# Reordering a state-space/FFN mix kernel: the second state's input projection before the first FFN output, one phase tile moved to VectorE, a constant for the warm-up

## Chip, cores, metric

One core of one Trainium2 chip. The metric is device time in microseconds (us) of the slowest (here the only) core; medians over several executions are quoted. Engine names in the profile: PE is TensorE, PEld its weight loads, DVE is VectorE, ACT is ScalarE, POOL is GpSimd, SP is SyncE; a "q" behind a name means that engine's instruction queue.

## The reference

```python
g = sigmoid((x * gate_w).sum(-1))                 # x: 2048 tokens x 448
Lam_bar = exp(dt * Lam); B_bar = (Lam_bar - 1) / Lam * B        # 448 complex states
h[t] = Lam_bar * h[t-1] + x[t] @ B_bar.T          # sequential over 2048 tokens
a = 2 * real(h @ C.T) + x * Dskip
b = silu(x @ w1) @ w2                             # 448 -> 1792 -> 448
out = g * a + (1 - g) * b                         # bfloat16
```

The kernel works on even and odd tokens apart (1024 pairs), in four chunks of 512 tokens for the FFN ("FFN1(c)" is x@w1 of chunk c, "FFN2(c)" the four 128-token rows q = 0..3 of silu(..)@w2) and in four tiles of states ("tile pt", "Bu(pt)" is its projection of x). The complex recurrence is turned into a real scan by multiplying with sine and cosine tables over the pair index. A table needs a *phase*: index times frequency, less its nearest integer.

## The kernel before

Each engine executes its own list in order; a tracker inserts semaphore waits from the declared reads and writes. So the order in which the program emits operations is the order on each engine. These are the parts that the change touches.

```python
        def phases(pt):                                   # GpSimd, two operations of 128x1024 f32
            f2 = "f2s" if pt == 3 else "f2"
            X, RR = phase(pt), G[:, pt % 2, :]
            T.op("pool", lambda e: e.tensor_scalar(X, IOTA[:, :], c1(f2, pt), 0.0, ALU.mult, ALU.add), ...)
            T.op("pool", lambda e: e.tensor_scalar(RR, X, 1.0, MAGIC, ALU.mult, ALU.add), ...)

        def phases2(pt):                                  # VectorE, one operation with two tensor inputs
            T.op("dve", lambda e: e.scalar_tensor_tensor(X, RR, MAGIC, X, ALU.subtract, ALU.subtract), ...)
        # ... (cut)
        ptt("lr", ...); ptt("li", ...); pts("nli", ...)   # 128x4 coefficients on VectorE; then "lis"
        phases(0)
        phases(3)
        phases2(0)
        phases(2)
        T.op("dve", ... tensor_copy(BT[0:64, 3, :], BT[64:128, 3, :]) ...)
        T.op("dve", ... tensor_copy(BR, BT[..., 384:448]) ...)          # TensorE needs BR for Bu(3)
        phases2(3)
        phases(1)
        swap_xr("dve", 1, 0)
        phases2(2)
        phases2(1)
        # ... (cut)
        def ffn2(c, q):                                   # 14 matmuls into one PSUM bank
            # c == 0: VectorE evicts it, bank * gate ratio + x * Dskip;  other chunks: ScalarE evicts
        # ... (cut: the main order)
        settle(); run(g2, 4)        # ScalarE: last SiLU, gate sums
        run(t3)                     # ScalarE: sine and cosine table of tile 3
        run(g2)                     # ScalarE: the other gate sums
        run(s0, 1)                  # VectorE: tile 0, turn and two scans
        run(g3)                     # VectorE: gate values for the first 1024 tokens
        for q in range(4):
            ffn2(0, q)              # TensorE; VectorE evicts
        run(s3, 1)                  # VectorE: a step of tile 3 (needs its tables)
        # ... (cut)
        bu(1, 0)
        bu(1, 1)
        for i, _ in enumerate(ffn1(2)):
```

## Time and profile before

Median 139.33 us (139.32 to 139.85). The profiled run took 139.70 us, of which 137.9 us are the span that the profile shows.

| engine | busy us | share of the span |
|---|---|---|
| PE | 133.1 | 97% |
| DVE | 121.7 | 88% |
| ACT | 94.8 | 69% |
| POOL | 31.1 | 23% |

The whole list of waits of TensorE in the kernel before (who waited, for whom; total us, times, longest):

```profile
PE ps L441 <- DVE Q L246: 1.0, 1, 1.0
PE ps L346 <- DVE IOTA L740: 0.9, 1, 0.9
PE ps L399 <- DVE XT L459: 0.2, 1, 0.2
```

The first and the last belong to the start. The middle one is the only hole later on. The timeline of TensorE around it (start us, us, engine, line, operation, output and input names, count; in brackets the idle time before it and what ended that):

```profile
36.75 10.77 PE L732 MATMUL ps<-W,AT 128*128 128x448 bf16 x56
47.45 2.55 PE L346 MATMUL ps<-XT,BT 64*128 64x512 bf16 x22
50.90 3.20 PE L346 MATMUL ps<-XT,BT 64*128 64x512 bf16 x28 [0.90 <-DVE IOTA L740]
```

FFN2(0) is the x56, Bu(1) follows. The 22 matmuls that start at 47.45 need 22 x 0.108 = 2.4 us, the next starts at 50.90: about 1.06 us is lost (the bracket says 0.90 because the end of a matmul is modelled). It waits for a PSUM bank that VectorE evicts late, since on VectorE the gate values and the evictions stand behind tile 0's two scans:

```profile
43.70 4.46 DVE L826 TENSOR_TENSOR_SCAN G<-P,Q 128x1024 f32<-128x1024 f32 x2
...
49.02 2.41 DVE L740 SCALAR_TENSOR_TENSOR IOTA<-ps,GT,XN 128x448 bf16<-128x448 f32 x4
```

The early phases in the kernel before, from the timelines of GpSimd and then of VectorE:

```profile
13.04 1.05 POOL L544 TENSOR_SCALAR G<-FP 128x1024 f32<-128x1024 f32 x1
14.26 2.07 POOL L542 TENSOR_SCALAR Q<-IOTA,P 128x1024 f32<-128x1024 f32 x1 [0.17 <-DVE P L600]
```

```profile
14.12 1.23 DVE L549 SCALAR_TENSOR_TENSOR FP<-G,FP 128x1024 f32<-128x1024 f32 x1
...
17.83 1.00 DVE L608 COPY BR<-BT 128x512 bf16<-128x512 bf16 x1
```

GpSimd's tensor_scalars of this size take 1.04 to 1.16 us when nothing holds them; the one that starts at 14.26, while a VectorE subtraction runs, takes 2.07. The copy of BR ends at 18.83; TensorE wants it at 19.61.

### The profile page before, as it was taken

What the parts mean: (1) busy time and instruction counts of PE and PEld (TensorE: products, weight loads), DVE (VectorE), ACT (ScalarE), POOL (GpSimd) and SP (SyncE); (2) the same over time, 40 slices, a digit from 0 to 9 for tenths busy, and PEclk for the clock granted to TensorE, in tenths of its full rate; (3) what the DMA queues carried; (4) which work ended last, traced back from release to release, by engine and by line L of the source; (5) the groups of instructions that cost most, each with busy time, mean ns of one, the idle gap of its engine ahead of it and who ended that gap; (6) DMA issues with size and microseconds to landing.
All of it is one profiled execution on the core that took longest, in us unless ns stands there. A gap on an engine that the chain in (4) does not pass through costs nothing.

```text
span 137.9 us, 2403 instructions
## 1 busy us (share of the span) xinstructions
PE 133.1 (97%) x957; PEld 65.4 (47%) x957; DVE 121.7 (88%) x151; ACT 94.8 (69%) x154; POOL 31.1 (23%) x36
## 2 busy tenths in 40 slices
PE   7999999999999979999999999999999999999992
PEld 7444444444455424444554444445555555555561
DVE  1269576999999999999999999999999999999763
ACT  0459899979999955899999258797214437789100
POOL 7105999950000000099940000000000000000000
PEclk9999999999999999999999999999999999999999
DMA  3999389899881500020200000000000000222124
GB/s 102 341 223 294 67 162 161 126 384 373 166 171 31 118 0 0 20 61 0 61 15 0 5 0 0 0 5 0 0 0 0 0 5 28 72 100 67 60 74 133
DMA packets 24321, 11.80 MB, mean 86 GB/s; under 512 B 16564, under 2 KB 23864, under 8 KB 24312
## 3 DMA queue, kind: packets, MB, share of 16 engines
q1 hardware_dynamic: 22724, 10.57, 31.5%
q10 hardware_dynamic: 1588, 1.11, 2.7%
q8 instruction: 7, 0.11, 0.4%
q14 instruction: 2, 0.02, 0.0%
HBM read 5.51 MB, written 1.84 MB: 53 GB/s over the span
## 4 chain that ended last, share of the span: by engine, by line
PE 60%; DVE 21%; SPq 12%; DMA 3%; issue 3%; DVEq 0%
PE ps L732 23%; PE ps L346 23%; PE ps L931 14%; SPq L231 10%; DVE G L826 3%; DVE Q L789 3%; DVE HS L792 3%; DMA XT<-in_A_x_dram 3%; SPq L228 2%; DVE G L792 2%; DVE FP L549 2%; DVE XN L590 2%; DVE CO L582 2%; DVE IOTA L740 1%; DVE FP L792 1%
## 5 line engine op out<-in xcount | busy, mean ns | idle before, releaser
L732 PE MATMUL ps<-W,AT 128*128 128x448 bf16 x224 | 42.9, 353 | 0.0
L346 PE MATMUL ps<-XT,W1E 64*128 64x512 bf16 x325 | 39.7, 376 | 0.0
L732 PEld LDWEIGHTS ps<-W,AT 128*128 128x128 bf16 x224 | 21.7, 98 | 21.2 <-ACT AT L417 0.8
L417 ACT ACTIVATE AT<-ps 128x1024 bf16<-128x1024 f32 x28 | 27.9, 1024 | 1.8 <-PE ps L346 1.8
L346 PEld LDWEIGHTS ps<-XT,W1E 64*128 64x128 bf16 x325 | 17.0, 94 | 19.1 <-DVE W1E L475 0.3
L346 PE MATMUL ps<-XT,BT 64*128 64x512 bf16 x168 | 20.0, 377 | 0.9 <-DVE IOTA L740 0.9
L745 ACT ACTIVATE BT<-ps,GT 128x448 bf16<-128x448 f32 x8 | 5.1, 633 | 13.1 <-PE ps L732 13.1
L778 ACT ACTIVATE VE<-ps 128x1024 bf16<-128x1024 f32 (+1 forms) x9 | 7.5, 836 | 8.8 <-PE ps L346 8.8
L346 PEld LDWEIGHTS ps<-XT,BT 64*128 64x128 bf16 x168 | 8.0, 94 | 11.3 <-DVE IOTA L740 1.4
L636 POOL TENSOR_TENSOR P<-P 128x4 f32<-128x4 f32 x5 | 5.6, 1122 | 29.1 <-DVE P L643 28.8
L931 PE MATMUL ps<-CO,VE 128*128 128x448 bf16 (+1 forms) x63 | 11.6, 332 | 0.0
L931 PE MATMUL ps<-CO,HS 128*128 128x448 bf16 x56 | 11.6, 353 | 0.0
L826 DVE TENSOR_TENSOR_SCAN G<-P,Q 128x1024 f32<-128x1024 f32 (+1 forms) x6 | 11.3, 1919 | 0.0
L346 PE MATMUL ps<-XR,W1E 64*128 64x512 bf16 x25 | 9.2, 376 | 0.0
L931 PEld LDWEIGHTS ps<-CO,VE 128*128 128x128 bf16 x63 | 6.1, 98 | 4.7
L792 DVE SCALAR_TENSOR_TENSOR HS<-VE,P,G 128x512 bf16<-128x512 bf16 (+1 forms) x10 | 8.1, 856 | 0.2
L931 PEld LDWEIGHTS ps<-CO,HS 128*128 128x128 bf16 x56 | 5.5, 98 | 5.1
L792 DVE SCALAR_TENSOR_TENSOR G<-VE,P,HS 128x1024 f32<-128x1024 bf16 (+1 forms) x5 | 7.5, 1495 | 0.1
L784 ACT ACTIVATE HS<-ps 128x1024 bf16<-128x1024 f32 (+1 forms) x9 | 7.5, 833 | 0.1
L789 DVE TENSOR_TENSOR Q<-G,COS 128x2048 bf16<-128x2048 f32 (+1 forms) x4 | 7.0, 1756 | 0.1
L789 DVE TENSOR_TENSOR Q<-G,SIN 128x2048 bf16<-128x2048 f32 (+1 forms) x4 | 7.0, 1750 | 0.0
L923 ACT ACTIVATE ps<-XN 128x448 f32<-128x448 bf16 x9 | 4.6, 539 | 1.4 <-DVE OT L955 1.4
(117 smaller groups left out, 186.6 us busy)
## 6 DMA issues: line engine op xcount, KB each, us to landing
W<-in_B_w_dram SPq DMA_DIRECT2D x1, 1568.0 KB, 11.9
XN<-in_A_x_dram SPq DMA_DIRECT2D x1, 896.0 KB, 7.9
out_dram<-OT SPq DMA_DIRECT2D x8, 112.0 KB, 1.7
out_dram<-TMPS SPq DMA_DIRECT2D x7, 112.0 KB, 1.7
W1E<-in_B_w_dram SPq DMA_DIRECT2D x3, 224.0 KB, 4.5
HS<-HS SPq DMA_DIRECT2D x4, 128.0 KB, 2.3
W1E<-in_B_w_dram SPq DMA_DIRECT2D x1, 384.0 KB, 6.1
XN<-in_A_x_dram SPq DMA_DIRECT2D x1, 384.0 KB, 5.9
```

The costliest lines, as they stand in the source:

```text
L231: return T.dma("sp", lambda e: e.dma_start_transpose(dst, src), reads=reads, writes=[key, *also], group=group)
L346: ins = pe.matmul(ps[:, bank, :], w(p, j), xh(odd, h, j, p), start=start and j == js[0], stop=stop and j == js[-1])
L417: T.op("act", lambda e: e.activation(a[:, fb:fb + n, :], ps[:, bank:bank + n, :], AF.Silu), reads=[f"ps{bank + i}" for i in range(n)], wri ...
L636: T.op("pool", lambda e: e.tensor_tensor(col(o), a, b, op), reads=ra, writes=[o])
L732: ins = pe.matmul(ps[:, bank, 0:D], a[:, fb, q * 128:(q + 1) * 128], W2[:, fb, :], start=(first and fb == 0), stop=(fb == NFB - 1), skip_g ...
L745: T.op("act", lambda e: e.activation(bs(tile), ps[:, bank, 0:D], AF.Copy, scale=sc), reads=[f"ps{bank}", "GT2" if h else "GRI"], writes=ks)
L778: T.op("act", lambda e: e.activation(VE[:, m0:m0 + n, hs], ps[:, b0:b0 + n, :], AF.Copy), reads=pe_, writes=[f"V{m}_{h}" for m in ms])
L784: T.op("act", lambda e: e.activation(HS[:, m0:m0 + n, 8 + h * 512:8 + (h + 1) * 512], ps[:, b1:b1 + n, :], AF.Copy), reads=po_, writes=[f" ...
L789: T.op("dve", lambda e: e.tensor_tensor(o, a, b, op), reads=reads, writes=writes)
L792: T.op("dve", lambda e: e.scalar_tensor_tensor(o, a, s, b, ALU.mult, ALU.add), reads=reads, writes=writes)
L826: T.op("dve", lambda e, c=c, init=init: e.tensor_tensor_scan(G[:, c, w], rb, Q1[:, c, w], init, ALU.mult, ALU.add), reads=[f"Q1{c}", "rr", ...
L931: ins = pe.matmul(ps[:, bank, c], state(kt, odd, m), CO[:, m, c], start=False, stop=(m == YB[-1]), skip_group_check=True)
```

## The change

Its intent: while VectorE is still in its scans, let TensorE do Bu(1), which ScalarE evicts, and do FFN2(0) after it, so that FFN2's banks need not be free so early. So that VectorE need not evict all four rows late, two rows (q = 2, 3) are *seeded*: ScalarE writes the scaled x into the bank first, the matmuls add to it, and ScalarE evicts. GpSimd is relieved of one of four tiles of phases. The warm-up matmuls read a constant that the program's preamble has written on GpSimd (at 0.36 us in the profile after), so that they need not wait for VectorE's memset. The diff is shortened; cuts are in brackets.

```diff
-NWARM = 24
+NWARM = 26
-        T.op("dve", lambda e: e.memset(Q1[:, 0, 0:128], 0.0), writes=["Q10"])
+        ones = nc.const_aps.tensor(1.0, [128, 128], BF16)
-                    ins = pe.matmul(ps[:, 7, 0:128], Q1[:, 0, 0:128], Q1[:, 0, 0:128], ...)
+                    ins = pe.matmul(ps[:, 7, 0:128], ones, ones, ...)
@@ phases (G's half by GP = (0, 0, 1, 1) instead of pt % 2)
-        def phases(pt):
+        def phases(pt, eng="pool"):
@@ order of phases, coefficients and copies
+        phases(0)
+        phases(2, "dve")
+        phases2(2)
+        phases(3)
+        phases2(0)
+        phases(1)
         ptt("lr", ...) ... lis
-        phases(0)
-        phases(3)
-        phases2(0)
-        phases(2)
+        ptt("rr", ...)
         (copies of BT and BR)
         phases2(3)
-        phases(1)
+        phases2(1)
         swap_xr("dve", 1, 0)
-        phases2(2)
-        phases2(1)
@@ ffn2
-            first = c != 2
+            first = c != 2 and (c, q) not in ((0, 2), (0, 3))
@@ main order
+        bu(1, 0)
+        run(g2, 2)
+        bu(1, 1)
+        run(g2, 1)
         settle()
-        run(g2, 4)
+        run(g2, 1)
         run(t3)
-        run(g2)
         run(s0, 1)
+        run(g3, 1)
+        for q in (2, 3):
+            ffn2_seed(q, q, 0)
+        ffn2(0, 0)
+        run(g2)
         run(g3)
-        for q in range(4):
-            ffn2(0, q)
         run(s3, 1)
+        for q in (1, 2, 3):
+            ffn2(0, q)
         (cut)
-        bu(1, 0)
-        bu(1, 1)
```

More of the change, by code (lines that the diff above doesn't have):

```diff
@@ L440, in mm @@
                 for _ in range(n):
-                    ins = pe.matmul(ps[:, 7, 0:128], Q1[:, 0, 0:128], Q1[:, 0, 0:128], start=True, stop=True)
+                    ins = pe.matmul(ps[:, 7, 0:128], ones, ones, start=True, stop=True)
                 return ins
-            T.op("pe", mm, reads=["Q10"], writes=["ps7"])
+            T.op("pe", mm, writes=["ps7"])
         warm(NWARM)
@@ L530, in gated_mix @@
         first = next(first)
-        ptt("rr", col("mag"), col("mag"), ALU.mult, ["mag"])
+        GP = (0, 0, 1, 1)
         def phase(pt):
@@ L537, in phase @@
             return Q3[:, :, :].rearrange("p a b -> p (a b)").bitcast(F32)
-        def phases(pt):
+        def phases(pt, eng="pool"):
             f2 = "f2s" if pt == 3 else "f2"
-            X, RR = phase(pt), G[:, pt % 2, :]
-            T.op("pool", lambda e: e.tensor_scalar(X, IOTA[:, :], c1(f2, pt), 0.0, ALU.mult, ALU.add),
+            X, RR = phase(pt), G[:, GP[pt], :]
+            T.op(eng, lambda e: e.tensor_scalar(X, IOTA[:, :], c1(f2, pt), 0.0, ALU.mult, ALU.add),
                  reads=["IOTA", f2], writes=[f"F{pt}"])
-            T.op("pool", lambda e: e.tensor_scalar(RR, X, 1.0, MAGIC, ALU.mult, ALU.add),
-                 reads=[f"F{pt}"], writes=[f"G{pt % 2}"])
+            T.op(eng, lambda e: e.tensor_scalar(RR, X, 1.0, MAGIC, ALU.mult, ALU.add),
+                 reads=[f"F{pt}"], writes=[f"G{GP[pt]}"])
         def phases2(pt):
-            X, RR = phase(pt), G[:, pt % 2, :]
+            X, RR = phase(pt), G[:, GP[pt], :]
             T.op("dve", lambda e: e.scalar_tensor_tensor(X, RR, MAGIC, X, ALU.subtract, ALU.subtract),
-                 reads=[f"F{pt}", f"G{pt % 2}"], writes=[f"F{pt}"])
+                 reads=[f"F{pt}", f"G{GP[pt]}"], writes=[f"F{pt}"])
         def tables(pt):
@@ L601, in gated_mix @@
              reads=["li"] + SGN, writes=["lis"])
-        phases(0)
-        phases(3)
-        phases2(0)
-        phases(2)
+        ptt("rr", col("mag"), col("mag"), ALU.mult, ["mag"])
         T.op("dve", lambda e: e.tensor_copy(BT[0:64, 3, :], BT[64:128, 3, :]), reads=BTK[2:4],
@@ L712, in xd, with ffn2_seed @@
             return XN[:, tile * D:(tile + 1) * D]
-        def ffn2_seed(q, off):
-            bank, tile = BANKS[(n_bank[0] + off) % len(BANKS)], 2 * q + 1
+        def ffn2_seed(q, off, odd=1):
+            bank, tile = BANKS[(n_bank[0] + off) % len(BANKS)], 2 * q + odd
             T.op("act", lambda e: e.activation(ps[:, bank, 0:D], xd(tile), AF.Copy,
@@ L738, in ffn2 @@
             ks = [f"BS{tile}"] + bsk(tile)
-            if c == 0:
+            if c == 0 and first:
                 T.op("dve", lambda e: e.scalar_tensor_tensor(
@@ L1006, in gated_mix @@
             run(g2, 1)
-        settle()
-        run(g2, 4)
-        run(t3)
         T.dma("act", lambda e: e.dma_start(XR[0:64, :], XT[64:128, 7, :]), reads=XO[0][3:] + XO[1][3:],
               writes=["XR0b", "XR1b"])
+        bu(1, 0)
+        run(g2, 2)
+        bu(1, 1)
+        run(g2, 1)
+        settle()
+        run(g2, 1)
+        run(t3)
+        run(s0, 1)
+        run(g3, 1)
+        for q in (2, 3):
+            ffn2_seed(q, q, 0)
+        ffn2(0, 0)
         run(g2)
-        run(s0, 1)
         run(g3)
-        for q in range(4):
+        run(s3, 1)
+        for q in (1, 2, 3):
             ffn2(0, q)
-        run(s3, 1)
         run(coef)
```

## The prediction

> **What bounds the kernel now.** TensorE. The page gives PE 133.1 of 137.9 us busy (97%). In the timeline, matmul starts from 8.2 us on follow at a fixed pitch (64-row pairs 0.108 us each, 128x448 ones 0.19 us), with one real hole: the wait list shows PE 0.9 us behind VectorE's L740 evictions of FFN2 of chunk 0. The timeline shows 22 Bu matmuls from 47.45, which need about 2.4 us, and the next at 50.90: about 1.07 us lost. Before 8 us: a clock that is slow until about 6.4 us (weight loads 0.42 us apart, then 0.22), and 1.03 us until the first matmul.
>
> **What the change does.**
> 1. Warm-up: no VectorE memset (0.86 to 0.97 us) before it; PE can start near 0.78 instead of 1.03. Two more 0.112 us matmuls fill that; the transposes still wait for x at 3.7. The Trainium skill (TensorE: Matmul & The Clock Gate, The HAM clock gate) has a free-running activity window of about 3.4 us, so the full clock may or may not come earlier. Worth 0 to 0.3 us.
> 2. Bu(1) before FFN2(0): evictions of Bu need ScalarE alone, so the 1.07 us hole goes. But rows 2 and 3 of FFN2 now need seeds that ScalarE writes after gate sums, 4 us of Bu evictions and three table activations (3.2 us). Adding trace durations: last SiLU at 38.4, Bu evictions done about 45.4, table done 49.5, first seed 50.1. PE is ready for row 2 at about 48.6 (first Bu pair held 0.4 us by a SiLU eviction ending at 36.48, Bu until 43.2, two rows of 2.67). Estimated new wait 1.5 us: this part saves 1.07 and costs about 1.9.
> 3. Tile 2's phases on VectorE. In before the GpSimd phase operations take 1.05 to 1.12 us alone and 2.07 to 2.10 when a VectorE operation with two inputs runs beside them; conversely a VectorE one of 1.22 takes 2.02 at 22.25. This agrees with the Trainium skill (SBUF — State Buffer, SBUF: two separate sides: an exclusive lock). So VectorE's two tensor_scalars, if they use both ports, and two subtractions alternate with GpSimd's. I estimate tile 0's phase at 17.5 to 18.2 instead of 15.35, and the BR copy at 20.5 to 21.8 instead of 18.83. ScalarE executes in order, so its SiLU and Bu evictions slip by 1 to 2 us; PE needs BR at 19.61. Estimated PE hole near 20 to 24 us: 1 to 2 us. VectorE's scan starts about 0.5 us earlier, but later than PE needs anyway.
>
> **Critical path.** After 50.9 us PE never waits in before, and VectorE leads PE at the end by 1.7 to 3.3 us, so PE's holes add one to one. Sum: -0.15 (clock) -1.07 +1.9 +1.5 = about +2. Because lock order and ScalarE's lag are estimates and could each vanish, I shade toward no stall, which would give 138.2.
>
> **Predicted:** 140.5 us, 8 in 10 between 138.1 and 142.4. Faster by over 2%: 0.03; within 2%: 0.80; slower: 0.17.
>
> **Right or wrong.** Step 1: first matmul near 0.8 us, weight loads at 0.22 us pitch sooner than 6.4. Step 2: no PE wait on the L740 evictions; a PE wait on ScalarE before the third FFN2 row, 1 to 2 us. Step 3: VectorE's new tensor_scalars interleave with GpSimd's, one of each pair lengthened; the first sine table starts near 17.5 to 18.2; a PE wait on VectorE's BR copy or on ScalarE near 20 to 24 us.
>
> **What would make it wrong.** VectorE's tensor_scalars not taking the lock, or winning every turn: hole 3 shrinks to 0.3. ScalarE less behind, so that seeds come in time: the result is 138.2. The second state's evictions or chunk 0's second VectorE eviction (now after tile 3's scan) holding banks of FFN1(2): slower.

## The result, and the profile after

Median 142.69 us (142.46 to 142.81) against 139.32 of before in the same rounds: slower, ratio 1.0232, 95% interval 1.0203 to 1.026. (A ratio here is the mean time of one kernel's fast runs over that of the other's of the same rounds, so it isn't quite the ratio of the medians quoted.) The profiled runs took 142.68 and 139.70 us, their spans are 140.9 and 137.9 us: 3.0 us apart.

TensorE's list of waits in the changed kernel (two of 0.2 us at the start are left out):

```profile
PE ps L345 <- DVE BR L613: 1.9, 1, 1.9
PE ps L735 <- ACT ps L719: 1.4, 1, 1.4
PE ps L442 <- PEq L1103: 0.8, 1, 0.8
PE ps L345 <- ACT AT L416: 0.4, 1, 0.4
...
```

The old wait for the evictions (DVE IOTA) is gone. In its place are three others: for the copy of BR, for a seed that ScalarE writes (line 719), and for a SiLU that still reads the bank which Bu(1) wants (line 416). The timeline of TensorE at these places:

```profile
17.54 2.11 PE L345 MATMUL ps<-XT,BT 64*128 64x512 bf16 x18
21.57 0.82 PE L345 MATMUL ps<-XT,BR 64*128 64x512 bf16 x6 [1.93 <-DVE BR L613]
...
37.34 0.81 PE L345 MATMUL ps<-XT,W1E 64*128 64x512 bf16 x6
38.50 1.04 PE L345 MATMUL ps<-XT,BT 64*128 64x512 bf16 x8 [0.35 <-ACT AT L416]
...
45.30 5.47 PE L735 MATMUL ps<-W,AT 128*128 128x448 bf16 x28
52.16 5.47 PE L735 MATMUL ps<-W,AT 128*128 128x448 bf16 x28 [1.39 <-ACT ps L719]
```

The sum can be drawn up from starts alone, so without modelled ends. The first FFN1 pair starts at 10.41 (10.54 before): -0.13. The step from the x18 to the BR matmuls is 4.03 us (1.95 before): +2.08. The six matmuls from 37.34 need 0.65 us, and the next comes 1.16 later: +0.51. The 28 matmuls of 0.191 us from 45.30 need 5.34 us, and the next comes 6.86 later: +1.52. The old hole: -1.06. Together +2.92; FFN2(1) starts at 68.25 instead of 65.25, so 0.08 is left over. From there to the end nothing differs.

Why was BR late? The timeline of VectorE in the changed kernel, and then that of GpSimd:

```profile
11.66 0.75 DVE L544 TENSOR_SCALAR FP<-IOTA,P 128x1024 f32<-128x1024 f32 x1
12.45 1.42 DVE L546 TENSOR_SCALAR G<-FP 128x1024 f32<-128x1024 f32 x1
13.90 3.07 DVE L551 SCALAR_TENSOR_TENSOR FP<-G,FP 128x1024 f32<-128x1024 f32 x2
16.90 1.06 DVE L500 TENSOR_TENSOR P<-P 128x4 f32<-128x4 f32 x2
17.99 1.03 DVE L497 TENSOR_SCALAR P<-P 128x4 f32<-128x4 f32 x1
...
20.60 0.92 DVE L613 COPY BR<-BT 128x512 bf16<-128x512 bf16 x1
```

```profile
11.66 1.66 POOL L544 TENSOR_SCALAR FP<-IOTA,P 128x1024 f32<-128x1024 f32 x1 [7.46 <-DVE P L500]
...
14.94 2.94 POOL L544 TENSOR_SCALAR Q<-IOTA,P 128x1024 f32<-128x1024 f32 x1 [0.17 <-POOL G L546]
17.96 1.04 POOL L546 TENSOR_SCALAR G<-Q 128x1024 f32<-128x1024 f32 x1
```

VectorE is hardly idle here, yet much of its busy time is being held up: the second tensor_scalar takes 1.42 us and overlaps GpSimd's first; a coefficient of 128x4 elements takes 1.03 us and ends with the GpSimd operation beside it. "Busy" in this view includes such a hold, the time in which an operation has started but is held up by the other engine. The BR copy ends at 21.52 and the matmuls start at 21.57.

Why was the seed late? ScalarE does the Bu evictions and three table activations first:

```profile
48.27 1.04 ACT L556 ACTIVATE SIN<-Q 128x1024 bf16<-128x1024 f32 x1
49.34 1.06 ACT L559 ACTIVATE Q<-Q 128x1024 f32<-128x1024 f32 x1
50.43 1.15 ACT L561 ACTIVATE COS<-Q,HP 128x1024 bf16<-128x1024 f32 x1
51.49 1.18 ACT L719 ACTIVATE ps<-XN,GT 128x448 f32<-128x448 bf16 x2
```

The gate values that a seed is scaled with are ready at 49.45 here, so ScalarE's own queue is what ends last.

### The profile page after: what moved, and what is told of

Same layout as the page of the kernel before. It is cut to its first block, busy times and chain, and to the rows that moved or that the text cites. A ratio compares the mean times of both kernels' runs of the same rounds, so it can differ in the third digit from the quotient of the medians.

```text
span 140.9 us, 2409 instructions
## 1 busy us (share of the span) xinstructions
PE 133.4 (95%) x959; PEld 65.2 (46%) x959; DVE 122.7 (87%) x150; ACT 97.2 (69%) x158; POOL 28.6 (20%) x34
## 4 chain that ended last, share of the span: by engine, by line
PE 71%; ACT 11%; DVE 10%; DMA 3%; issue 1%; SPq 1%; DVEq 0%
PE ps L345 30%; PE ps L735 27%; PE ps L934 14%; DMA R<-in_A_Lambda_re_dram 3%; DVE FP L551 2%; ACT AT L416 2%; ACT VE L781 2%; ACT HS L787 2%; ACT CO L686 2%; DVE P L497 1%; SPq L228 1%; DVE P L500 1%; DVE G L546 1%; DVE TMPS L958 1%; DVE BT L611 1%
## 5 line engine op out<-in xcount | busy, mean ns | idle before, releaser
L639 POOL TENSOR_TENSOR P<-P 128x4 f32<-128x4 f32 x5 | 4.6, 921 | 32.6 <-DVE P L646 32.3
L792 DVE TENSOR_TENSOR Q<-HS,COS 128x1024 bf16<-128x1024 bf16 (+1 forms) x5 | 4.5, 902 | 1.7 <-ACT COS L561 1.6
```

What stands on the lines that cost most here:

```text
L639: T.op("pool", lambda e: e.tensor_tensor(col(o), a, b, op), reads=ra, writes=[o])
L792: T.op("dve", lambda e: e.tensor_tensor(o, a, b, op), reads=reads, writes=writes)
```

## The experiments

**A start that varies.** The profiled runs of the kernels below don't all start alike: the first FFN1 pair, a fixed point of the program, starts anywhere from 9.82 to 10.75 us in the fast profiles, with and without the new warm-up. This blurs medians by some tenths of a microsecond. So beside the median I give the stretch from that point to the end of the profiled span, "mark to end". It is one run each, and spans are printed to 0.1 us, so hundredths mean nothing here; kernels with the same holes (e3 and e8, e4 and e7 below) agree well within that. In before it is 137.9 - 10.54 = 127.36, in the changed kernel 140.9 - 10.41 = 130.49 (+3.13).

| run | what it is | median us (before) | ratio, 95% interval | mark to end us | against before |
|---|---|---|---|---|---|
| changed kernel | all three parts | 142.69 (139.32) | 1.0232, 1.0203 to 1.026 | 130.49 | +3.13 |
| e1_warm | warm-up part alone | 139.27 (139.31) | 1.0012, 0.9992 to 1.0033 | 127.38 | +0.02 |
| e2_phases | phases part alone | 140.45 (139.31) | 1.0082, 1.0068 to 1.0097 | 128.42 | +1.06 |
| e3_bufirst | Bu-first part alone | 140.52 (139.31) | 1.0088, 1.0066 to 1.0111 | 128.43 | +1.07 |
| e12_bc | both of these | 142.38 (139.44) | 1.0214, 1.0193 to 1.0236 | slow profile | |
| e4_alldve | before, all phases on VectorE | 138.64 (139.31) | 0.9958, 0.9939 to 0.9977 | 126.30 | -1.06 |
| e9_alldve_dummy | e4 and unrelated GpSimd work | 143.93 (139.44) | 1.0346, 1.0312 to 1.038 | 130.97 | +3.61 |
| e8_after_alldve | changed kernel, all phases on VectorE | 140.42 (139.41) | 1.0074, 1.0054 to 1.0095 | 128.44 | +1.08 |
| e11_seeds_before_tables | e3, tables behind the seeds | 145.59 (139.44) | 1.0449, 1.0416 to 1.0482 | 134.42 | +7.06 |
| e10_gate_first | e3, gate and seeds early | 139.16 (139.44) | 0.9977, 0.9953 to 1.0002 | 126.85 | -0.51 |
| e5_noseed | e3 without seeds | 139.04 (139.41) | 0.9976, 0.9957 to 0.9996 | 127.21 | -0.15 |
| e6_all | warm-up, e4 and e5 together | 139.11 (139.41) | 0.9981, 0.9962 to 0.9999 | 126.80 | -0.56 |
| e7_warm_alldve | warm-up and e4 together | 138.61 (139.41) | 0.9953, 0.9925 to 0.9981 | 126.32 | -1.04 |

All gave the right result. The profile of e11 is the slowest of its four runs, at a lower clock (see below), so its +7.06 is more than its median shows.

### The three parts alone, and two together

e1_warm is the first hunk of the diff put into the kernel before, e2_phases the hunks of phases and their order, e3_bufirst the hunks of ffn2 and of the main order, e12_bc the last two sets.

> Only the warm-up part (constant operand, 26 matmuls) put into the kernel before. My theory: matmuls from 8 us on start about 0.13 us earlier, as in the changed kernel, but the VectorE evictions of FFN2 of chunk 0 end when they did, so the hole near 50 us grows by as much (from 1.07 to about 1.2 us) and the time stays within 0.1 us of before, 139.3. Rival (the three parts add up): 0.13 us or more is gained, 139.2 or less, and the hole is unchanged.

Measured: 139.27, no difference. So the time came out as expected, but the reason given was not seen. The first matmul starts at 0.82 instead of 1.03. The profiled run happens to have an early start (mark at 9.82), VectorE's chain moved with it, and the wait for its evictions was 0.6 us by the wait list, not longer than 0.9. Part of that early start went into a wait for w1's transfer (0.2 us in the list, 0.34 by starts). Since profiles without the new warm-up have marks from 9.97 on, the early start can't be credited to it: the five fast profiles with it have a mean mark of 10.17, the eight without 10.32, each spread over more than 0.5 us.

> Only the phases part. My theory: BR's copy ends near 21.5 us and TensorE has a hole of about 2.1 us before the BR matmuls; but TensorE then comes later to the banks that VectorE frees near 49 to 50 us, so the old 1.07 us hole vanishes. Net about +1.0 us: 140.3. Rival (the parts add up): +2.1 us, 141.4, both holes present.

Measured: 140.45, +1.06 by mark to end, as the first theory says. All of TensorE's waits:

```profile
PE ps L346 <- DVE BR L612: 1.9, 1, 1.9
PE ps L441 <- DVE Q L246: 1.0, 1, 1.0
PE ps L399 <- DVE XT L459: 0.2, 1, 0.2
```

The new hole is there and the old one isn't: TensorE arrives about 2 us later at the banks, when VectorE has already freed them.

> Only the Bu-first part with its ScalarE seeds. My theory: the 1.07 us hole goes, a hole of about 0.5 us before the first Bu matmuls (bank still read by a SiLU) and one of about 1.5 us before the third FFN2 row (seed) come: +1.0 us, about 140.3. Rival: the seed wait in the changed kernel is a knock-on of the late BR copy, which delayed ScalarE; then without the phases part there is no seed wait and the time falls by about 0.6 to 1.0 us, to 138.3 to 138.7.

Measured: 140.52, +1.07 by mark to end. The seed wait is there without the phases part, in the same size. The rival falls. TensorE's timeline at the seed:

```profile
42.76 5.47 PE L732 MATMUL ps<-W,AT 128*128 128x448 bf16 x28
49.62 5.47 PE L732 MATMUL ps<-W,AT 128*128 128x448 bf16 x28 [1.39 <-ACT ps L716]
```

> Bu first with seeds, and the phases part, without the warm-up part. My theory: the old hole of 1.07 us can be saved only once, so both parts' new holes (2.1 before BR, 0.5 and 1.5 around Bu and the seeds) less one old hole: about +3.2 us, 142.5. Rival (the parts' own differences, +1.2 and +1.1, add up): +2.3 us, 141.6.

Measured: 142.38 median of the fast runs (one run of 144.83 is slow, and the profile fell into it, so it isn't compared; as a hint only, that profile's mark is at 12.56, and from there to the end it took 130.5 us, as the changed kernel did). That is 2.94 us over before, where the parts' own medians add to 2.35; by mark to end the changed kernel costs 3.13 and its parts add to 2.15. The missing microsecond is the old hole, which each part fills when it is alone and which only one can fill when they are together. So two costs that look like 1.1 us each are some 2.1 us each, less 1.06 once.

### Why BR was late: the shared port, or more work on VectorE

e4_alldve, put into the kernel before, gives all eight of GpSimd's phase operations to VectorE. The diff shows the order beside that of the changed kernel:

```diff
-        phases(0)
-        phases(2, "dve")
-        phases2(2)
-        phases(3)
-        phases2(0)
-        phases(1)
+        phases(0, "dve")
+        phases2(0)
+        phases(2, "dve")
+        phases2(2)
         (coefficients, copies of BT and BR)
+        phases(3, "dve")
         phases2(3)
+        phases(1, "dve")
         phases2(1)
```

> The kernel before with all four tiles' phases on VectorE and none on GpSimd, tile 0 first, tile 2 second, then the small coefficients and the BT and BR copies: VectorE has two more tensor_scalars ahead of BR than in the changed kernel. My theory (the shared port made them late): with GpSimd silent each tensor_scalar takes about 0.65 us and each subtraction 1.2, tile 0's sine starts by 16.0 us, BR ends near 18.2, no hole near 20 us; the first scan starts near 23.5 instead of 25.45, so that the evictions near 49 us end earlier and the 1.07 us hole goes too: about 138.3. Rival (VectorE simply has more work ahead of BR): BR ends later than in the changed kernel, 22 us or more, the hole before BR is 2.5 us or more, and the time is 140.5 or more.

Measured: 138.64, faster than before by 0.7 us in the median (its interval is clear of 1) and 1.06 by mark to end. VectorE's timeline up to BR, and TensorE's Bu(1):

```profile
12.53 0.69 DVE L545 TENSOR_SCALAR G<-FP 128x1024 f32<-128x1024 f32 x1
13.26 1.23 DVE L550 SCALAR_TENSOR_TENSOR FP<-G,FP 128x1024 f32<-128x1024 f32 x1
...
17.06 0.23 DVE L499 TENSOR_TENSOR P<-P 128x4 f32<-128x4 f32 x2
...
18.21 0.29 DVE L610 COPY BR<-BT 128x512 bf16<-128x512 bf16 x1
```

```profile
47.41 5.57 PE L346 MATMUL ps<-XT,BT 64*128 64x512 bf16 x50
```

With two tensor_scalars *more* ahead of it, BR ends at 18.50, three microseconds sooner than in the changed kernel. The same operations take 0.69 instead of 1.42, 0.23 instead of 1.06 and 0.29 instead of 0.92. TensorE's waits list no hole after the start, because VectorE's first operation on tile 0 after the phases starts at 24.15 instead of 25.45 and the two scans at 42.40 instead of 43.70, so that the evictions near 49 us begin at 47.72 instead of 49.02.

Without GpSimd's phases there is neither port sharing nor a wait for GpSimd's data. e9_alldve_dummy separates the two: e4 and, on GpSimd, six operations of the same kind that nobody waits for.

```diff
+        for _ in range(6):
+            T.op("pool", lambda e: e.tensor_scalar(scratch, IOTA[:, :], c1("f2", 0), 0.0, ALU.mult, ALU.add),
+                 reads=["IOTA", "f2"], writes=["TMP0", "TMP1", "TMP2"])
         phases(0, "dve")
```

> All phases on VectorE as in the run before, and GpSimd is given six tensor_scalars of the same size (128x1024 f32) on a scratch tile in the same stretch; nothing on VectorE waits for their results. My theory (the shared port itself, not the wait for GpSimd's data): VectorE's operations of 0.7 and 1.2 us are held in turn, each by about 0.7 to 1 us, BR's copy ends 4 to 6 us later than the 18.4 us of all-VectorE, TensorE has a hole of 3 to 5 us before BR, time 141.5 to 143.5. Rival (in the changed kernel VectorE only waited for GpSimd's data): no VectorE operation is lengthened, time about 138.6.

Measured: 143.93, half a microsecond over the expected band. The profiled run (143.30 us, granted clock 1.00) lies inside it; the three others took 143.91 to 144.89 us at mean clocks of 0.988 to 0.976, so part of the excess may be clock, but no trace of them is kept. In the profile the wait for BR is 3.1 us. VectorE's timeline, then GpSimd's:

```profile
12.26 1.42 DVE L545 TENSOR_SCALAR G<-FP 128x1024 f32<-128x1024 f32 x1
13.72 2.02 DVE L550 SCALAR_TENSOR_TENSOR FP<-G,FP 128x1024 f32<-128x1024 f32 x1
15.67 1.61 DVE L543 TENSOR_SCALAR FP<-IOTA,P 128x1024 f32<-128x1024 f32 x1
```

```profile
11.48 10.37 POOL L600 TENSOR_SCALAR TMPS<-IOTA,P 128x1024 f32<-128x1024 f32 x6 [7.28 <-DVE P L499]
```

No VectorE operation depends on these six, and yet 0.69 becomes 1.42 and 1.22 becomes 2.02. So the operations hold each other up by being there at the same time. This agrees with the exclusive lock on the pair of ports that GpSimd and VectorE share, as the Trainium skill has it (SBUF — State Buffer, section "SBUF: two separate sides"), and the sizes fit roughly: the tensor_scalar that starts at 12.26 is held 0.73 us, and GpSimd's first operation, alone in the timeline from 11.48 to 13.14, has 0.88 us left.

e8_after_alldve is the changed kernel with e4's order of phases.

> The changed kernel with all four tiles' phases on VectorE and GpSimd silent in that stretch. My theory: the 2.1 us hole before BR goes; the seed wait of 1.4 to 1.5 us and the 0.4 to 0.5 before Bu stay, the old hole does not come back: about 142.69 - 2.1 = 140.5. Rival (ScalarE's lag and so the seed wait came from the late phases): the seed wait shrinks as well, 139 or less.

Measured: 140.42, as expected. Mark to end is 128.44, that of e3_bufirst (128.43), and the seed wait is again 1.4 us. The phases part accounts for the wait for BR and for nothing else; the seed wait isn't its consequence.

### Why the seed was late

In e3_bufirst both things that a seed needs come near 49 us: ScalarE gets to it at 48.94, behind the tables of tile 3, and the gate values it scales with are ready on VectorE at 48.53, behind tile 0's scans. e11_seeds_before_tables takes away the first alone, in e3_bufirst:

```diff
         run(g2, 1)
-        run(t3)
         run(s0, 1)
         run(g3, 1)
         for q in (2, 3):
             ffn2_seed(q, q, 0)
+        run(t3)
```

> Bu first with seeds as in the change, only tile 3's three tables moved behind the two seeds on ScalarE. My theory (two queues end together): the seed now waits for VectorE's gate values behind the scans (48.5 us with the early start, 49.1 without) and starts only 0.2 to 0.4 us sooner, the wait before the third row is 1.0 to 1.2 us instead of 1.4, and tile 3's step starts 3 us later: 140.1 to 140.6. Rival (the tables alone hold the seeds): seeds near 46, no wait, 138.9.

Measured: 145.59. The time is far off what I expected, the seeds are not: they start at 48.78 instead of 48.94 (0.47 us sooner, counted from the mark), behind the gate values of VectorE, and the wait for them is 0.9 us. ScalarE's timeline has them waiting for the last gate operation of VectorE (line 703):

```profile
48.78 1.19 ACT L716 ACTIVATE ps<-XN,GT 128x448 f32<-128x448 bf16 x2 [2.64 <-DVE GT L703]
```

What I had noted but not followed to the end is that tile 3's step on VectorE waits for the tables (4.0 us), and the eviction of FFN2's row 1 stands behind that step, at 60.10. FFN1(2) wants its bank, and TensorE idles 3.4 us:

```profile
60.84 1.46 PE L346 MATMUL ps<-XT,W1E 64*128 64x512 bf16 x6 [3.42 <-DVE IOTA L740]
```

Within this hole its clock drops. Stretches of the profile (us; length, PE busy, ..., granted clock, DMA share, GB/s):

```profile
56.00:58.00 2.00, 1.42 (x14) 0.45 (x10) 1.97 (x2) 1.94 (x9) 0.00 (x0) 1.00 0.00 0
58.00:60.80 2.80, 0.00 (x0) 0.00 (x0) 2.80 (x5) 2.80 (x6) 0.00 (x0) 0.84 0.19 44
60.80:62.80 2.00, 1.96 (x10) 0.75 (x12) 1.97 (x3) 0.38 (x1) 1.71 (x2) 0.50 0.30 70
```

In finer stretches the granted clock is 0.50 from 59.9 to 66.7 us, which costs about 3 us more: from mark to end this run is 5.99 us over e3_bufirst, of which the hole is 3.4, less 0.5 of seed wait saved. So in this run the hole cost nearly twice its length. The other three runs had mean clocks of 0.987 and 0.988 instead of 0.976, so about half as much clock was lost (an estimate: 0.012 of 143.4 us against 0.024 of 144.7), and took 145.14 to 145.79 us instead of 146.45. The Trainium skill gives about 3.4 us of idleness as what sends the clock back to half (TensorE: Matmul & The Clock Gate, section "What's actually happening"); here it fell about 2.5 us after the last matmul, which ended at 57.4. In the profiled run of e9_alldve_dummy a hole of 3.14 us left the granted clock at 1.00, and so did those of 1.9 us in the changed kernel; but the three other runs of e9 had mean clocks below 0.99. How long a hole the clock survives stays open.

e10_gate_first takes away both causes: the gate sums on ScalarE before Bu's evictions, the gate values on VectorE between the turn and the scans, the tables behind the seeds, and the evictions of rows 0 and 1 before tile 3's step.

```diff
         bu(1, 0)
-        run(g2, 2)
+        run(g2, 4)
         bu(1, 1)
-        run(g2, 1)
         settle()
-        run(g2, 1)
-        run(t3)
+        mid.append(lambda: run(g3, 1))      # executed inside the turn, ahead of the scans
         run(s0, 1)
-        run(g3, 1)
         for q in (2, 3):
             ffn2_seed(q, q, 0)
+        run(t3)
         ffn2(0, 0)
+        ffn2(0, 1)
```

> Bu first with seeds, phases as before; the gate sums before Bu's evictions on ScalarE, the six small gate operations on VectorE before its two scans, tile 3's tables after the seeds, and VectorE's two FFN2 evictions before tile 3's step. My theory (the seeds are late because of two queues, ScalarE's tables and VectorE's scans, both ending near 49 us): seeds near 45.5 to 46.8, the wait before FFN2's third row goes, only the 0.4 to 0.5 us before Bu stays: about 138.7. Rival (the seeded row waits for something else, as PSUM banks or the cost of ScalarE writing PSUM): the wait stays over 1 us, 140 or more.

Measured: 139.16; mark to end -0.51, which is the old hole filled (-1.06) and the wait for the SiLU's bank paid (+0.5). The seeds start at 45.62; of TensorE's waits after the start only the 0.4 us for the SiLU's bank is left in its list, and FFN2(0) is one unbroken x56 from 43.54 on.

```profile
43.54 10.77 PE L732 MATMUL ps<-W,AT 128*128 128x448 bf16 x56
```

```profile
45.62 1.22 ACT L716 ACTIVATE ps<-XN,GT 128x448 f32<-128x448 bf16 x2
```

So the two queues were the cause, and writing a seed as such isn't. (VectorE's queue alone was not taken away in a run of its own; e11 shows what it holds once the tables are gone.) The median is 0.5 us over my figure; its profiled run has the latest start of all fast ones (mark at 10.75).

e5_noseed leaves the seeds out of e3_bufirst; VectorE evicts rows 0 and 1 before tile 3's step and rows 2 and 3 behind it.

```diff
-        for q in (2, 3):
-            ffn2_seed(q, q, 0)
         ffn2(0, 0)
+        ffn2(0, 1)
         run(g2)
         run(g3)
         run(s3, 1)
-        for q in (1, 2, 3):
+        for q in (2, 3):
             ffn2(0, q)
```

> Bu first, but FFN2's four rows all start from zero and are evicted by VectorE as before, two ahead of tile 3's step and two behind it; phases and warm-up as before. My theory: no seed wait; the old hole is gone, 0.4 to 0.5 us before the first Bu matmuls stay, the banks of the last two rows come free just in time: 138.7, at most 0.3 us more. Rival (Bu first as such costs): 140 or more.

Measured: 139.04, at the upper end of what I had allowed (139.0), -0.15 by mark to end. There is no seed wait; 0.36 us before Bu stay, and 0.23 us for VectorE's last evictions come at 57.77. Bu first as such doesn't cost; it gains less than it could.

### Two candidates

> A candidate: warm-up part, all phases on VectorE, Bu first without seeds. My theory: all three big holes gone, the 0.4 to 0.5 us before Bu stays, the start 0.1 us earlier: 138.4. Rival: the early start of Bu hits another bank or ScalarE's queue, over 139.

Measured: 139.11. By mark to end -0.56, as the sum of its holes says: the big ones are gone, the wait for the SiLU's bank remains. The median is above my figure and in the rival's band, but the list shows none of the rival's waits; as marks vary by up to 0.9 us between profiles, the median alone can't decide.

> A candidate: warm-up part and all phases on VectorE, the order of Bu and FFN2 as before. My theory: no hole after 8 us; the gain of the earlier start (0.1 to 0.5 us) is now not eaten up by the hole near 50 us unless VectorE's evictions are late by it: 138.3 to 138.6. Rival: the hole near 50 us comes back by what the start gains, 138.64 as without the warm-up part.

Measured: 138.61, within 0.03 us of e4's 138.64, so the warm-up part again gave nothing; TensorE's list of waits has nothing after the start, so the rival's hole isn't there either. By mark to end it equals e4_alldve. Both beat both kernels by keeping the old order of Bu and FFN2: once VectorE starts tile 0 and its scans 1.3 us sooner there is no hole left that Bu first could fill, and Bu first has its own 0.5 us.

## Why the prediction was wrong

- **What bounds the kernel**: right. TensorE's holes add one to one (sum above, 2.92 of 3.0 us).
- **Step 1, the warm-up**: the first matmul started at 0.82 (0.78 predicted), the mark came 0.13 us earlier. In the changed kernel's profile the pitch of weight loads shortens near 5.7 us instead of 6.4, but the start varies by more than this, and alone the part gave nothing (139.27).
- **Step 2, Bu first**: right in mechanism and size. Old hole -1.07 predicted, -1.06 measured; new waits 0.4 + 1.5 predicted, 0.51 + 1.52 measured. e10_gate_first and e5_noseed show the cause.
- **Step 3, phases on VectorE**: right in mechanism (e4_alldve, e9_alldve_dummy), too small in size. "Estimated PE hole near 20 to 24 us: 1 to 2 us", with 1.5 in the sum, was 2.08 us. The copy of BR ended at 21.52, inside the range predicted, and TensorE starts 0.05 us later; measured from the 19.5 us at which it would have started, that is 2.08. The estimate of tile 0's phase, 17.5 to 18.2, was too late: it ended at 16.97, since the second subtraction followed the first at once although a GpSimd operation had been waiting since 14.94. ScalarE's delay, the other half of this step, was real (the sine started at 17.01 instead of 15.98) but in that stretch never the last thing that TensorE waited for.
- **The step that failed**: the discount at the end of the critical-path sum, "Because lock order and ScalarE's lag are estimates and could each vanish, I shade toward no stall", on top of one term that was too small, step 3's hole before BR. The terms, as they stood, added to about +2.2, so 141.5 us, and I gave 140.5 with an upper end of 142.4. The runs showed the stalls in full: the hole before BR was 2.08 us instead of 1.5, the two waits around Bu and the seeds 2.03 instead of 1.9. The median was missed by 2.2 us. Of these, 1.0 is the shading, and 0.8 is what the profiled runs show beyond the sum (2.98 instead of 2.2: 0.58 for BR, 0.13 for the two waits around Bu and the seeds, the rest small change). The last 0.4 is not in the profiles: the profiled run of before (139.70) was 0.37 us slower than the median of before, while the changed kernel's was typical. That would fit a late start in that one run, since starts vary by as much; no trace of the other runs shows it, and it stays open.
- **The interplay**: not said in the prediction, and it explains why the parts looked harmless. Each part alone costs 1.06 us, since it also fills the old hole. Together they cost 3.13.

## What to carry to other kernels

A hole on the bounding engine can be filled only once: test the parts of a change together, and expect the second one to show its full cost. Moving work from GpSimd to VectorE needn't run it in parallel when both use their shared port: here moving one tile of four cost a hole of 2.1 us, and moving all four gained 1.06. Look in a trace for operations that take up to twice their time alone. Where durations from a trace give a sum, don't trim it because its terms are estimates; widen the range instead.

## What the Trainium skill lacked or had wrong

- SBUF — State Buffer ("SBUF: two separate sides") states the lock and which operations take it, and the runs agree (a tensor_scalar of 0.69 us took 1.42, a subtraction of 1.22 took 2.02, six unrelated GpSimd operations took 10.37 us). On who goes first, its section "Who interferes with whom" says that issue order decides. The runs bear this out only in part: in e9_alldve_dummy a tensor_scalar that started at 15.67, with a GpSimd operation waiting since 14.77, was held (1.61 instead of 0.75 us); but in the changed kernel a subtraction that started at 15.76 was not held (1.21 us), although a GpSimd operation had been waiting since 14.94.
- The same page names no size and has no example of a small operation. Here one was held like a large one: coefficients of 128x4 elements on VectorE, 0.15 to 0.2 us when free, took about 1.0 us beside a GpSimd operation (1.03 for one tensor_scalar in the changed kernel).
- VectorE: DVE Perf Modes ("The perf-mode tier table") has no line for scalar_tensor_tensor. Here 128x1024 f32 in SBUF took 1.22 us when free; a tensor_scalar of the same size took 0.69 to 0.75, which fits the table's two elements per cycle.
- TensorE: Matmul & The Clock Gate ("What's actually happening") has the clock fall after about 3.4 us of idleness. In e11_seeds_before_tables it fell about 2.5 us after the last matmul, within a hole of 3.42 us, and stayed at 0.50 for 6.8 us. After a hole of 3.14 us in the profiled run of e9_alldve_dummy it stayed at 1.00, while three other runs of e9 had mean clocks of 0.976 to 0.988.
